# An FFT filter with a gated feed-forward: the inverse transform's first chunk opened a slot sooner, its rows in two parts, and fewer matmul columns

## The chip, the cores and the metric

The kernel runs on one core of a Trainium2 chip. The metric is the device time of one execution in microseconds (us); the time of a kernel is the median of its runs. The trace is that of one profiled execution, and its times count from the start of its span. Engines have short names: PE is the matmul engine (PEld its weight loads), DVE, ACT and POOL the vector, scalar and GpSimd engines, SP the engine that issues nearly all transfers.

## The reference, cut to what matters

```python
# x [1, 2048, 1024], w_r and w_i [2048, 513], w1 [1024, 3584], w2 [3584, 1024]
xn = _layernorm(x)
X = jnp.fft.rfft2(xn, axes=(-2, -1)) * (w_r + 1j * w_i)
s = jnp.fft.irfft2(X, s=(S, D), axes=(-2, -1))
h = _silu(jnp.einsum("bsd,df->bsf", xn, w1))
g = _silu(jnp.einsum("bsf,fd->bsd", h, w2))
return x + s * g
```

## The kernel before, in words

PE runs one long stream. First come the 112 tiles of the first feed-forward matmul (`mm1`, tile `pa`), then the second (`mm2`, tile `pb`, L584 to L586): seven products m of a Strassen-like scheme by eight row tiles j, each in two halves k of 21 matmuls of 512 columns. Every value is kept as two float16 halves, so each product is three passes: high by high, high by low, low by high. The spectral filter goes between these matmuls as background work. `work()` is called after each half of `mm2`; one such call is a slot here. In a slot the background list `bg` may take a step, then `wq` (`w2_gen`) prepares a piece of w2: a transfer into `jr`, a second one into a spare part of a `w` tile, an addition on POOL (L457), a split on ACT and DVE (L284, L287). A background step that yields `PAUSE` ends its slot; after other steps the list goes on while DVE's estimated clock is less than 1 us ahead of PE's. `defer(n, fn)` runs `fn` n ticks later; there is one tick a slot, ahead of its work.

The background around the change is, in order: `f_gen`, the filter along the sequence, sixteen units u, whose results `zq` go to DRAM as `zd[c]`, one quarter q after every four units (`low_z`, L1101 for even c, L1104 for odd c); `edge_gen`, which treats the columns that the units leave out, with nine fp32 matmuls into `eps` (L1231 to L1233), and writes `zps` through DRAM (L1287, L1285); `switch(B, open_i, 5, lag=2)`, which lets two slots go by, closes the filter's pool, calls `open_i` and then lets slots go by until the fifth `PAUSE` is spent; and `i_gen(c)` for c in `IORDER` = 1, 3, 0, 2, the four chunks of the inverse transform.

`open_i` calls `load_i(1)`: for an odd chunk four transfers of 512 KB bring `zd[c]` to the tile `zt`, two for each half of the partitions (L1308), then one brings the constants `kk` (L1312). `i_gen(1)` begins with `edge_in(1)`, a DVE copy of `zps` into the first column of every block of `zt` (L1319), and a `PAUSE`. Its steps i = 0 to 5 then interleave `mat(g)` (24 matmuls of 128 columns into `iu`, L1350, from `zt` and `kk`; for even chunks L1358), `post(g)` (ACT and DVE) and `split(g)`. `mat(0)` is emitted in step 0, `mat(1)` in step 1, `mat(2)` and `mat(3)` at the end of steps 1 and 2, after their `PAUSE`. Group g reads two of the eight blocks l of each row of `zt`. When all four are through, `load_i` of the next chunk is called and `mat2(p)`, p = 0 to 3, runs: 24 matmuls each into `id` (L1439), whose bank is read by `bfly(p)` (L1448 to L1453).

SP issues transfers in program order. The second matmul's rows `ht` are issued by the half, two at the start of each j: the second half of the tile two further on and the first half of the one after that. The lines that the prediction needs most:

```python
add(bg, switch(B, open_i, 5, lag=2))          # in the order loop
src = zd[c].rearrange("(m e) r q h x -> r m e (q h) x", e=2)      # load_i, odd c
nc.sync.dma_start(dst[64 * r:64 * r + 64, e], src[r, :, e])       # L1308
(nc.vector if c == IORDER[0] else nc.gpsimd).tensor_copy(zt[:, :, :, :, 0, 0], zps[:, :, c])   # L1319
for r, cols in enumerate((slice(0, 130), slice(0 if g == 0 else 127, 256))):                   # mat2
```

## Time and profile before

| | us |
|---|---|
| median of 3 runs | 1208.4 (1207.18 to 1208.95) |
| profiled execution, its own time | 1207.29 |
| span of its trace | 1205.5 |
| PE busy in the span | 1195.1 (99%) |
| DVE busy | 1009.7 (84%) |
| ACT busy | 511.6 (42%) |
| POOL busy | 210.2 (17%) |

The profiled execution lies 1.1 us below the median and 0.1 us above the fastest run; 1.8 us of it lie outside the span. PE busy is the union of its matmuls, whose recorded ends overlap, so a matmul's cost is read from the distance between starts, or from the chain view, which splits the time without overlap. A wait is the idle time of an engine ahead of an instruction, with what ended it.

### The profile page before, as it was taken

The page shows a single profiled execution, that of the slowest core. Times are in us where ns is not written, and L with a number is a line of the kernel's source. Part 1 is how long each engine was busy: PE and PEld are TensorE (multiplying, and loading weights), DVE is VectorE, ACT ScalarE, POOL GpSimd, SP SyncE. Part 2 cuts the span into 40 slices and gives each one's busy share as a digit, 9 for nine tenths or more (in the row PEclk, how much of TensorE's full clock was granted, in tenths as well). Part 3 has the DMA queues.
Part 4 walks back from the last instruction along what each step waited for, and adds up shares of the span by engine and source line. Part 5 has one row for each costly group of instructions (what it writes and reads, how often), then busy time and mean ns, then how long its engine had stood idle before and what let it go on. Part 6 is the DMA issues. An engine that isn't in the chain of part 4 may idle for free.

```text
span 1205.5 us, 18361 instructions
## 1 busy us (share of the span) xinstructions
PE 1195.1 (99%) x6600; PEld 597.1 (50%) x6600; DVE 1009.7 (84%) x1971; ACT 511.6 (42%) x698; POOL 210.2 (17%) x297
## 2 busy tenths in 40 slices
PE   8999999999999999999999999999999999999998
PEld 5544445444544544444444444445455545555555
DVE  7778986996799598669968999999279898998696
ACT  7775654366466463445524233132032222343212
POOL 2330041102402300411100111125031231100000
PEclk9999999999999999999999999999999999999999
DMA  8788698589989976889989999993997989989577
GB/s 263 182 192 213 199 268 242 173 248 281 294 251 278 275 227 197 195 197 205 183 234 246 284 239 261 237 305 131 261 333 219 367 308 329 363 319 343 175 242 267
DMA packets 279540, 302.24 MB, mean 251 GB/s; under 512 B 47956, under 2 KB 206932, under 8 KB 278548
## 3 DMA queue, kind: packets, MB, share of 16 engines
q1 hardware_dynamic: 275848, 291.69, 81.1%
q0 software_dynamic: 3312, 9.24, 4.5%
q8 instruction: 52, 0.85, 0.3%
q14 instruction: 40, 0.33, 0.1%
q10 hardware_dynamic: 288, 0.13, 0.0%
HBM read 183.94 MB, written 110.77 MB: 244 GB/s over the span
## 4 chain that ended last, share of the span: by engine, by line
PE 93%; DVE 3%; DMA 3%; issue 1%; SPq 1%; ACT 0%; POOL 0%; ACTq 0%; DVEq 0%
PE pa L500 48%; PE pb L584 12%; PE pb L585 12%; PE pb L586 12%; PE id L1439 2%; PE fx L1070 2%; DMA ht<-hd 2%; PE iu L1358 1%; PE iu L1350 1%; PE fa L837 1%; PE fa L838 1%; PE fa L839 1%; DMA w<-in_B_w_dram 0%; DVE Z L1192 0%; SPq L1104 0%
## 5 line engine op out<-in xcount | busy, mean ns | idle before, releaser
L500 PE MATMUL pa<-xnT,w 128*128 128x512 f16 x2688 | 584.0, 379 | 0.0
L500 PEld LDWEIGHTS <-w 128*128 128x128 f16 x2688 | 261.6, 98 | 311.9 <-issue 0.3
L584 PE MATMUL pb<-w,ht 128*128 128x512 f16 (+2 forms) x812 | 300.4, 372 | 1.0 <-DMA ht<-hd 1.0
L585 PE MATMUL pb<-w,ht 128*128 128x512 f16 (+2 forms) x812 | 300.4, 372 | 0.0
L586 PE MATMUL pb<-w,ht 128*128 128x512 f16 (+2 forms) x812 | 300.3, 372 | 0.0
L509 ACT ACTIVATE h<-pa,s 128x512 f32<-128x512 f32 x112 | 75.9, 681 | 153.4 <-PE pa L500 112.8
L586 PEld LDWEIGHTS <-ht 128*128 128x128 f16 x812 | 79.5, 98 | 91.0
L584 PEld LDWEIGHTS <-ht 128*128 128x128 f16 x812 | 79.5, 98 | 87.7 <-DMA ht<-hd 1.1
L585 PEld LDWEIGHTS <-ht 128*128 128x128 f16 x812 | 79.5, 98 | 86.5
L284 ACT ACTIVATE w<-jr,sc 128x512 f16<-128x512 f32 x98 | 67.5, 712 | 64.6 <-POOL jr L457 60.4
L287 DVE SCALAR_TENSOR_TENSOR hoone<-h,hs,hoone 128x2048 f16<-128x2048 f32 x28 | 65.6, 2342 | 17.0 <-ACT hoone L284 17.0
L287 DVE SCALAR_TENSOR_TENSOR w<-jr,sc,w 128x512 f16<-128x512 f32 x98 | 78.0, 803 | 0.0
L1192 POOL TENSOR_TENSOR Z<-yb 128x32 f32<-128x32 f32 x64 | 34.9, 573 | 224.9 <-DVE yb L1169 224.9
L284 ACT ACTIVATE hoone<-h,hs 128x2048 f16<-128x2048 f32 x28 | 55.9, 1997 | 18.4 <-DMA hd<-hoone 18.4
L457 POOL TENSOR_TENSOR jr<-jr,w 128x512 f32<-128x512 f32 x28 | 38.8, 1387 | 123.8 <-DMA w<-in_B_w_dram 75.9
L1092 ACT ACTIVATE zq<-Z,zs 128x1024 f16<-128x1024 f32 x16 | 18.4, 1148 | 91.5 <-DVE Z L1192 54.3
L287 DVE SCALAR_TENSOR_TENSOR hosum<-hr,hs,hosum 128x1536 f16<-128x1536 f32 x28 | 50.7, 1811 | 7.2 <-ACT hosum L284 7.2
L284 ACT ACTIVATE hosum<-hr,hs 128x1536 f16<-128x1536 f32 x28 | 43.9, 1569 | 20.5 <-DMA hd<-hosum 12.1
L539 DVE TENSOR_TENSOR hr<-h 128x1024 f32<-128x1024 f32 x28 | 34.1, 1218 | 18.3 <-ACT h L509 18.0
L678 ACT ACTIVATE pl<-pl,c 128x512 f32<-128x512 f32 (+2 forms) x28 | 17.4, 655 | 72.7 <-DVE pl L654 42.4
L284 ACT ACTIVATE w<-w1r,rs 128x1024 f16<-128x1024 f32 x28 | 32.0, 1143 | 27.8 <-DVE w L287 23.5
L1192 DVE TENSOR_TENSOR Z<-yb 128x128 f32<-128x128 f32 (+1 forms) x128 | 42.3, 398 | 0.0
(246 smaller groups left out, 1520.4 us busy)
## 6 DMA issues: line engine op xcount, KB each, us to landing
ht<-hd SPq DMA_DIRECT2D x112, 448.0 KB, 6.5
hd<-hoone SPq DMA_DIRECT2D x28, 1024.0 KB, 8.6
hd<-hosum SPq DMA_DIRECT2D x28, 768.0 KB, 5.5
w1r<-in_B_w_dram SPq DMA_DIRECT2D x28, 512.0 KB, 6.6
w2m<-in_B_w_dram SPq DMA_DIRECT2D x28, 512.0 KB, 6.4
jr<-in_B_w_dram SPq DMA_DIRECT2D x56, 256.0 KB, 6.2
ws<-wd SPq DMA_DIRECT2D x42, 256.0 KB, 4.4
jr<-ws SPq DMA_DIRECT2D x42, 256.0 KB, 6.2
```

What stands on the lines that cost most here:

```text
L284: nc.scalar.activation(hi, raw, AF.Copy, scale=scale)
L287: nc.vector.scalar_tensor_tensor(lo, raw, scale, hi, op0=OP.mult, op1=OP.subtract)
L457: nc.gpsimd.tensor_tensor(raw[n], raw[n], more.pop(n), op=OP.add)
L500: nc.tensor.matmul(ps, w[:, wh, d], xt[:, xh, d], start=(n == 0), stop=(n == 23))
L509: nc.scalar.activation(hq[:, 2 * (c % 2) + f % 2], ps, AF.Silu, scale=s1[:, f:f + 1])
L539: tt(sums[:, 0:2], hq[:, 0::2], hq[:, 1::2], op=OP.subtract)
L584: nc.tensor.matmul(ps, hh[:, 0], w[:, 0], start=first, stop=False)
L585: nc.tensor.matmul(ps, hh[:, 0], w[:, 1], start=False, stop=False)
L586: nc.tensor.matmul(ps, hh[:, 1], w[:, 0], start=False, stop=last)
L1070: nc.tensor.matmul(o, k[:, c, kh], v[:, c, vh], start=(n == 0), stop=(n == 2))
L1192: eng.tensor_tensor(Z[:, ns, pos], x0[:, :, ls], x1[:, :, ls], op=o_)
L1439: nc.tensor.matmul(ps[:, g, cols], us[g][:, uh, 4 * r + p], C["ci"][:, ch, g, r, cols], start=(r == 0 and n == 0), stop=(r == 1 and n == 2 ...
```

## The change

- The wait behind `open_i` is 4 in place of 5: the first chunk's `edge_in`, `mat(0)`, `mat(1)`, `mat(2)` with their `post` and `split` steps are emitted one slot sooner. `open_i` itself, and so the first load, stays in its slot.
- Behind step 2 of the first chunk stands one more `PAUSE`, so that `mat(3)` and all that follows keep their slots.
- `zd[c]` of an odd chunk is laid out with the two halves b of the eight blocks apart. It is written by four transfers a quarter as before, each now of one half h (runs of 512 bytes in place of 1024). `load_i` issues `kk` first, then four transfers of 256 KB for b = 0, and by `defer(2, ...)` four more for b = 1. Groups 0 and 1 read b = 0, groups 2 and 3 read b = 1; `edge_in` writes b = 0 only.
- `mat2` leaves out columns: 130 become 129 for groups 1 to 3 in the first row part, and the low constants' pass of group 0's second part has 129 in place of 256.
- The nine `eps` matmuls become three, of 72, 24 and 24 columns.

```diff
@@ -174,7 +174,7 @@
     rd = [[dp.tile([256, 1024], F32, name=f"rd{side}_{j}") for j in range(4)] for side in range(2)]
     rows4 = [[t.rearrange("(a c) (q r k) -> a c q r k", c=4, q=4, r=2) for t in half] for half in rd]
     axis = [dp.tile([2, 4096], F32, name=f"axis{c}") for c in range(2)]
-    zd = [dp.tile([128, 2, 4, 2, 512] if c % 2 else [128, 4, 2, 1024], F16, name=f"zd{c}") for c in range(4)]
+    zd = [dp.tile([128, 2, 2, 4, 2, 256] if c % 2 else [128, 4, 2, 1024], F16, name=f"zd{c}") for c in range(4)]
     zpd = dp.tile([128, 4, 2, 4, 2], F16, name="zpd")
     SETS = ("sum_0", "sum_1", "sum_d"), ("one_0", "dif_1", "dif_0", "one_3")
     hds = {(k, g): dp.tile([128, 4 * len(m), NP, 2, 128], F16, name=f"hd_{k}_{g}") for k, m in enumerate(SETS) for g in range(2)}
@@ -1100,8 +1100,9 @@
                 for c in range(0, 4, 2):
                     defer(1, lambda c=c: nc.sync.dma_start(zd[c][:, q], zv[:, :, c]))
                 for c in range(1, 4, 2):
-                    for r in range(2):
-                        defer(1, lambda c=c, r=r: nc.sync.dma_start(zd[c][:, r, q], zv[:, :, c, 512 * r:512 * r + 512]))
+                    for h in range(2):
+                        defer(1, lambda c=c, h=h: nc.sync.dma_start(
+                            zd[c][:, :, :, q, h].rearrange("m r b x -> m (r b) x"), zv[:, h, c].rearrange("m (k x) -> m k x", k=4)))
 
         load_w(0)
         high_v(0)
@@ -1227,10 +1228,11 @@
             g.tensor_copy(r0[:, n, 1:4], xv[:, n, 0, 3:0:-1])
         yield 1
         ps = pf.tile([128, 512], F32, name="eps", tag="ff")
-        for n in range(3):
-            nc.tensor.matmul(ps[:, n * 32 + 8:n * 32 + 32], perm[:, 0], rv[:, n, 1:4].rearrange("m q a r -> m (q a r)"), start=True, stop=True)
-            nc.tensor.matmul(ps[:, n * 32:n * 32 + 8], perm[:, 1], rv[:, n, 0].rearrange("m a r -> m (a r)"), start=True, stop=False)
-            nc.tensor.matmul(ps[:, n * 32:n * 32 + 8], perm[:, 2], r0[:, n].rearrange("m a r -> m (a r)"), start=False, stop=True)
+        p3 = ps[:, 0:96].rearrange("m (n x) -> m n x", n=3)
+        r3 = rv.rearrange("m n q a r -> m n (q a r)")
+        nc.tensor.matmul(p3[:, :, 8:32], perm[:, 0], r3[:, :, 8:32], start=True, stop=True)
+        nc.tensor.matmul(p3[:, :, 0:8], perm[:, 1], r3[:, :, 0:8], start=True, stop=False)
+        nc.tensor.matmul(p3[:, :, 0:8], perm[:, 2], r0.rearrange("m n a r -> m n (a r)"), start=False, stop=True)
         yield 1
         rr = piece(96).rearrange("m (n a r) -> m n a r", n=3, a=16)
         nc.scalar.activation(rr.rearrange("m n a r -> m (n a r)"), ps[:, 0:96], AF.Copy)
@@ -1300,23 +1302,29 @@
 
     def load_i(c):
         zt = C["p"].tile([128, 8192], F16, name=f"zt{c}", tag="zt", bufs=1)
+        k = C["p"].tile([128, 2064], F16, name=f"kk{c}", tag="kk", bufs=1)
         if c % 2:
-            src = zd[c].rearrange("(m e) r q h x -> r m e (q h) x", e=2)
-            dst = zt.rearrange("m (e k x) -> m e k x", e=2, k=8)
-            for r in range(2):
-                for e in range(2):
-                    nc.sync.dma_start(dst[64 * r:64 * r + 64, e], src[r, :, e])
+            nc.sync.dma_start(k, ki[c])
+            src = zd[c].rearrange("(m e) r b q h x -> r m e b (q h x)", e=2)
+            dst = zt.rearrange("m (e b x) -> m e b x", e=2, b=2)
+
+            def part(b):
+                for r in range(2):
+                    for e in range(2):
+                        nc.sync.dma_start(dst[64 * r:64 * r + 64, e, b], src[r, :, e, b])
+
+            part(0)
+            defer(2, lambda: part(1))
         else:
             nc.sync.dma_start(zt.rearrange("m (q h x) -> m q h x", q=4, h=2), zd[c])
-        k = C["p"].tile([128, 2064], F16, name=f"kk{c}", tag="kk", bufs=1)
-        nc.sync.dma_start(k, ki[c])
+            nc.sync.dma_start(k, ki[c])
         C["z"][c], C["k"][c] = zt, k
 
     def edge_in(c):
         zt = C["z"][c]
         if c % 2:
-            zt = zt.rearrange("m (e q h l i) -> m e q h l i", e=2, q=4, h=2, l=8)
-            (nc.vector if c == IORDER[0] else nc.gpsimd).tensor_copy(zt[:, :, :, :, 0, 0], zps[:, :, c])
+            zt = zt.rearrange("m (e b q h l i) -> m e b q h l i", e=2, b=2, q=4, h=2, l=4)
+            (nc.vector if c == IORDER[0] else nc.gpsimd).tensor_copy(zt[:, :, 0, :, :, 0, 0], zps[:, :, c])
         else:
             zt = zt.rearrange("m (q h r l i) -> m q h r l i", q=4, h=2, r=2, l=8)
             nc.gpsimd.tensor_copy(zt[:, :, :, :, 0, 0], zp[:, c].rearrange("m r q h -> m q h r"))
@@ -1329,7 +1337,7 @@
         yield PAUSE
         zt, k = C["z"].pop(c), C["k"].pop(c)
         if c % 2:
-            zt = zt.rearrange("m (e q h l i) -> m e q h l i", e=2, q=4, h=2, l=8)
+            zt = zt.rearrange("m (e b q h l i) -> m e b q h l i", e=2, b=2, q=4, h=2, l=4)
             k = k.rearrange("m (h y) -> m h y", h=2)[:, :, 0:1024].rearrange("m h (e q x) -> m e q h x", e=2, q=4)
         else:
             zt = zt.rearrange("m (q h r l i) -> m q h r l i", q=4, h=2, r=2, l=8)
@@ -1346,7 +1354,7 @@
                     for q in range(4):
                         o = ps[:, 512 * e + 128 * q:512 * e + 128 * q + 128]
                         for n, (zh, kh) in passes:
-                            lhs = zt[:, e, q, zh, ls].rearrange("m l i -> m (l i)")
+                            lhs = zt[:, e, g // 2, q, zh, slice(2 * (g % 2), 2 * (g % 2) + 2)].rearrange("m l i -> m (l i)")
                             nc.tensor.matmul(o, lhs, k[:, e, q, kh], start=(n == 0), stop=(n == 2))
                 return
             width, second = (129, 127) if c else (128, 128)
@@ -1434,8 +1442,9 @@
         def mat2(p):
             ps = pt.tile([128, 4, 256], F32, name=f"id{c}_{p}", tag="ft")
             for g in range(4):
-                for r, cols in enumerate((slice(0, 130), slice(0 if g == 0 else 127, 256))):
+                for r, span in enumerate((slice(0, 129 if g else 130), slice(127 if g else 0, 256))):
                     for n, (uh, ch) in passes:
+                        cols = slice(127, 256) if r and ch else span
                         nc.tensor.matmul(
                             ps[:, g, cols], us[g][:, uh, 4 * r + p], C["ci"][:, ch, g, r, cols],
                             start=(r == 0 and n == 0), stop=(r == 1 and n == 2), skip_group_check=True)
@@ -1509,6 +1518,8 @@
             if c == IORDER[0] and i == 1:
                 nc.sync.dma_start(C["ci"], ci)
             yield PAUSE if i <= 3 else 3.9
+            if c == IORDER[0] and i in (2,):
+                yield PAUSE
             if 1 <= i <= 2:
                 mat(i + 1)
         if c != IORDER[-1]:
@@ -1678,7 +1689,7 @@
                 max_job = add(xq, w2max_gen())
                 f_job = add(bg, switch(A, open_f, 1, max_job))
                 add(bg, f_gen())
-                add(bg, switch(B, open_i, 5, lag=2))
+                add(bg, switch(B, open_i, 4, lag=2))
                 for k in IORDER:
                     add(bg, i_gen(k))
             if left == 2 * LAST + 3:
```

## Rows read from the trace of the kernel before

**Rows 1.** The page's first part: busy time of each engine.

```profile
PE 1195.1 (99%) x6600; PEld 597.1 (50%) x6600; DVE 1009.7 (84%) x1971; ACT 511.6 (42%) x698; POOL 210.2 (17%) x297
```

**Rows 2.** Waits of PE, whole span: total us, times, longest us.

```profile
PE tp L805 <- ACT x L788: 1.6, 2, 1.4
PE tp L803 <- ACT x L788: 1.4, 1, 1.4
PE spin L1622 <- POOL ones L1614: 1.0, 1, 1.0
PE pb L584 <- DMA ht<-hd: 1.0, 1, 1.0
PE iu L1350 <- DMA kk<-in_kc_dram: 0.6, 1, 0.6
```

**Rows 3.** Stretches: us, busy PE, PEld, DVE, ACT, POOL (instructions), PEclk, DMA share, GB/s.

```profile
860.00:875.00 15.00, 15.00 (x71) 6.86 (x70) 1.35 (x2) 0.72 (x1) 1.05 (x1) 1.00 1.01 225
875.00:900.00 25.00, 23.49 (x180) 13.38 (x178) 18.06 (x41) 8.37 (x13) 8.23 (x6) 1.00 0.93 348
900.00:1100.00 200.00, 200.00 (x1272) 106.08 (x1271) 185.17 (x394) 60.22 (x114) 29.80 (x25) 1.00 0.90 320
```

**Rows 4.** Timeline of PE, 814 to 817: start us, us, line, [idle before, releaser].

```profile
814.70 0.30 PE L1231 MATMUL eps<-edge,perm 128*128 128x24 f32 x2
...
816.62 0.38 PE L584 MATMUL pb<-w,ht 128*128 128x512 f16 x1
```

**Rows 5.** Timeline of PE, 876 to 884: the first chunk's matmuls.

```profile
876.26 1.50 PE L1350 MATMUL iu<-kk,zt 128*128 128x128 f16 x24 [0.55 <-DMA kk<-in_kc_dram]
878.71 0.39 PE L584 MATMUL pb<-w,ht 128*128 128x512 f16 x1 [0.96 <-DMA ht<-hd]
...
883.26 1.50 PE L1350 MATMUL iu<-kk,zt 128*128 128x128 f16 x24
```

**Rows 6.** Chain that ended last, in pieces: start us, us, what.

```profile
813.55 1.31 PE fx L1070 x12
...
883.42 1.34 PE iu L1350 x24
...
926.86 1.53 PE id L1439 x24
```

**Rows 7.** Timeline of SP's issues, 846 to 866.

```profile
846.01 5.02 SPq L1104 DMA_DIRECT2D zd<-zq  x4
...
858.11 2.94 SPq L1308 DMA_DIRECT2D zt<-zd  x4
861.09 0.66 SPq L1312 DMA_DIRECT2D kk<-in_kc_dram  x1
...
865.55 2.58 SPq L560 DMA_DIRECT2D ht<-hd  x2
```

**Rows 8.** One line's issues and landings: L1308 (858 to 861), L560 (867.8), L447 (834.9).

```profile
L1308 SPq DMA_DIRECT2D zt<-zd x4: 476/594/1125, 858.1 to 859.9; - x4
...
DMA to landing us min/median/max: 9.6/12.4/15.2
...
L560 SPq DMA_DIRECT2D ht<-hd x1: 326/326/326, 867.8 to 867.8; - x1
DMA to landing us min/median/max: 12.0/12.0/12.0
...
L447 SPq DMA_DIRECT2D jr<-in_B_w_dram x1: 333/333/333, 834.9 to 834.9; - x1
DMA to landing us min/median/max: 3.1/3.1/3.1
```

**Rows 9.** Transfers in stretches 849:855, 326.4:328 and 862:872: packets, MB, mean rate.

```profile
DMA packets 1683, 2.33 MB, mean 388 GB/s; under 512 B 108, under 2 KB 1072, under 8 KB 1683
...
DMA packets 1031, 0.54 MB, mean 338 GB/s; under 512 B 3, under 2 KB 1026, under 8 KB 1031
...
DMA packets 322, 2.00 MB, mean 200 GB/s; under 512 B 60, under 2 KB 60, under 8 KB 97
```

**Rows 10.** Timelines of DVE and POOL, 837 to 876: the edge copy, one unit's Z.

```profile
875.51 0.21 DVE L1319 COPY zt<-zps 128x16 f16<-128x16 f16 x1 [12.02 <-DMA jr<-in_B_w_dram]
...
838.64 2.61 DVE L1192 TENSOR_TENSOR Z<-yb 128x128 f32<-128x128 f32 x8
...
837.49 2.23 POOL L1192 TENSOR_TENSOR Z<-yb 128x32 f32<-128x32 f32 x4 [0.74 <-DVE yb L1169]
```

## The prediction

> **What bounds the kernel now.** I read the busy times first: PE is busy 1195.1 of 1205.5 us and the next engine, DVE, 1009.7 [rows 1]. So the end moves only by PE work that goes and by PE idle time that goes. The list of PE's waits comes next: five entries. Three of them, 4.0 us, wait for the first layer norm and for the constant of the warm-up matmuls, which the change does not touch; the other two, 0.96 for `ht` and 0.55 for `kk`, are the only ones behind these [rows 2]. The timeline of PE puts both at one place, the first chunk of the inverse: `mat(0)` starts at 876.26 after 0.55 of idle time and the `pb` behind it at 878.71 after 0.96 [rows 5]. The stretches tell why: from 860 to 875 DVE works 1.35 us of 15 and ACT 0.72, while the DMA engines are taken all the time and yet move only 225 GB/s; from 900 on PE is full and DVE is at 185 of 200 [rows 3]. So there are three things to price: 1.51 us of idle time at 876, the matmul columns, and what moving `mat(0)` does at the place where the data are late.
>
> **Columns of `mat2`.** A matmul of 256 columns costs 1.31/12 = 109 ns in the chain, one of 128 columns 1.34/24 = 56 ns [rows 6], so 128 columns are 53 ns, 0.417 a column. One `mat2` loses 127 columns in one matmul and one column in nine, 136 columns, 57 ns. There are sixteen: **0.91 us**. `mat2` itself supports it: 3489 columns take 1.53 us [rows 6], 0.44 a column. PE is full around them [rows 3], so all of it reaches the end, unless DVE, which is at 93% there, becomes what PE waits for; today no PE wait names it [rows 2].
>
> The Trainium skill speaks against this term: TensorE: Matmul & The Clock Gate, section Back-to-back issue gap, gives a sustained spacing of about 81 ns at 128 columns and 131 at 512. By it 127 columns would be worth some 16 ns (my estimate from its two points), and the term 0.3 us. The trace disagrees, with 56 ns at 128.
>
> **Edge matmuls.** The nine fill PE from 814.70 to 816.62 [rows 4], 213 ns each whether 24 or 8 columns wide, so the fixed part sets their price. Three cost 0.64: **1.28 us** saved; were the one of 72 columns twice as dear, 1.07. I take 1.28. Their reader is POOL work that is not on the path.
>
> **The slot.** `mat(0)` was wanted when PE came free, at 876.26 - 0.55 = 875.7. A slot is 878.71 to 883.26, 4.55 us [rows 5], of which 0.02 is the reading. A slot sooner and with the edge saving ahead of it, PE comes free for it at 875.7 - 4.53 - 1.28 = **869.9**. The planner's condition does not hold it back: DVE does next to nothing in those slots [rows 3].
>
> When are its data there? The chain to them does not start at PE: before the rows can be read `zq` must be written, and SP's issues of that run from 846.0 on, with `zt` at 858.1 and `kk` at 861.1 [rows 7]. I assume that these times stay. The four `zt` pieces land 9.6 us after the first issue, at 867.7, to 15.2 after the last, at 875.1 [rows 8]: 2.46 us a piece of 512 KB, about 200 GB/s, as the packets of 862 to 872 also give [rows 9]. The edge copy then runs at 875.51, after DVE had waited 12.02 us, for 0.21 [rows 10]. `kk` comes in at about 876.2, where the stall ends, 1.1 us behind the last piece [rows 5].
>
> In the new order the queue turns to this load at 867.7 - 2.46 = 865.3. `kk` is first, 1.1; the four half pieces are 1.23 each, 4.9; the edge copy and what lies around it took 0.65 after the last landing. That makes 871.9. To it comes the price of the 512-byte runs: the window with the `zd` writes moves 388 GB/s, windows of nearly nothing but 512-byte packets 338 [rows 9], so the 1 MB of the last quarter takes 3.1 in place of 2.7 us, 0.4 more, on the path that sets `zt`'s issue; three earlier quarters are off it. This gives 872.3, and as the upper end 873, if the runs lose nearly three times that, since the window holds other packets too. Lower end: `kk` at 388 GB/s and half of `zt` at 213, from the issue at 858.1 on plus a lone landing of 3.1 [rows 8, 9], 868.1. Nearest is the loaded queue, since it is taken all through this stretch [rows 3]; I take **872.0**. PE, free at 869.9, then stands for 2.1 us, ends 0 to 3.1.
>
> **The `ht` stall.** The matmul that waited at 878.71 needs the transfer issued at 865.55, behind all of `zt` and `kk` [rows 5, 7]. Now half of `zt` lies behind it. It follows the half pieces (871.4), `jr` and `w`, and comes in at about 874 (the next `ht` landed at 867.8 + 12.0 = 879.8, so 1.1 a piece [rows 8]); it is wanted behind `mat(1)`, at 872.0 + 1.34 + 4.53 + 1.34 = 879.2. **0.96 is gone**, and so is the old 0.55. The second part of the rows is queued behind `ht`: 874 + 1.1 + 4.9, some 880 to 881; `mat(2)` wants it a slot behind `mat(1)`, near 883.8. The margin of 3 us is the cover of that step; without it each late us is a us.
>
> What else is queued: the edge copy now stands a slot sooner in DVE's order and holds the w2 split and an evacuation behind it until 872, as it held them until 875.5; PE did not wait for these then. The c = 3 load, 70 us later, is split as well; its first matmul then waited for nothing [rows 2]. The empty slot costs nothing on PE, which has `pb` in it.
>
> **Sum.** 0.91 + 1.28 + 0.96 + 0.55 - 2.1 = 1.6 us saved. The profiled execution of 1207.29 would become 1205.7; it lies 1.1 below the median, so the median of 1208.4 becomes **1206.8**. That is 0.13%, inside the 0.2% (2.4 us) that a measurement of this kernel can tell from no change. The point of it is that moving `mat(0)` takes back most of what the halved load gives.
>
> **Rivals.**
>
> *The rows are there when PE asks.* With data at 870 or sooner nothing is lost: 3.7 us, 1204.7; from 871.2 on downward the gain is over 2.4. For it: the half pieces are shorter packets and SP may be held less ahead of them. Against: the load in the queue from 846 on. The same time comes out if the change does not do what it says, the planner skipping a slot so that `mat(0)` stays where it was: wanted at 874.4, data at 872.0, no stall. Together 0.31.
>
> *The edge copy or `mat(0)` waits for both parts* (slower). The second part is issued ahead of the edge copy in program order, and lies between its rows in memory. If the dependence were drawn by spans, `mat(0)` would wait for 881 + 0.65, a stall of 11.7 us: 1216.4. It decides from a stall of 6.1 on (3.7 + 2.4). Against it: POOL's Z writes every eighth row between DVE's, is emitted behind them, and yet starts at 837.49, ahead of DVE's at 838.64 [rows 10], so interleaved regions are told apart. 0.04.
>
> *Each of the added transfers pays for itself* (slower). If the half pieces did not follow each other but each took near the 3.1 us of a lone 256 KB transfer [rows 8], part 0 would end 4 x 3.1 = 12.4 after 866.4, `mat(0)` at 879.5, a stall of 9.6, 1214.3. Against: in the loaded queue 448 KB follow in 1.1. 0.05. The Trainium skill has the rule behind this in SBUF — State Buffer, section The DMA setup-cost knee: about 2 us a transfer whatever its size; by its formula a half piece is 2.6 us, which would make it 1212. The trace agrees for a lone transfer and not for a queue of them.
>
> *Narrow matmuls save nothing.* If spacing hardly fell below 256 columns, 0.6 less, 1207.4. 56 against 109 ns speak against it. 0.04.
>
> **How the numbers follow.** Forecast, with stalls of 1.4 to 3.1 around it: 0.53. With the narrow-matmul rival the same side has 0.57. Faster 0.31; slower 0.04 + 0.05, and 0.03 for a second part that is late at `mat(2)` by more than 5 us over its margin: 0.12. The range takes in the case of no stall, with the 0.3 by which medians of three may lie lower, and on the other side a saving of nothing (873 and a share of the costs not seen) with the spread of 0.9 of the runs above: 1204.4 to 1209.3.
>
> **What would show it.** The time from the last `zq` write to `zt`'s issue about 0.4 longer; three `eps` matmuls in 0.64; `mat2` in 1.47; `mat(0)` at about 872 with PE idle some 2 us before it, and the edge copy its releaser; no idle time at the `pb` behind `mat(1)` or at `mat(2)`. I am wrong if `mat(0)` starts without a wait, if it waits past 873, or if PE waits at a place where it had none.

## The result, and the profile after

The changed kernel takes 1209.26 us (median of 18 runs, 1205.32 to 1215.03) where the kernel before takes 1206.53 beside it (18 runs, 1205.28 to 1209.46). The ratio is 1.0026 with an interval of 1.0018 to 1.0034: slower by about 3.1 us by the ratio (2.7 between the medians), where 1.6 us of gain were forecast. The median lies just under the upper end of the predicted range; the sign is wrong.

The profiled execution of after took 1209.53, its span is 1207.6, 2.1 longer than that of before. Its busy row, which answers to [rows 1]:

```profile
PE 1192.1 (99%) x6588; PEld 594.7 (49%) x6588; DVE 1007.4 (83%) x1971; ACT 511.7 (42%) x698; POOL 210.2 (17%) x295
```

and PE's waits, as in [rows 2]:

```profile
PE iu L1358 <- DVE zt L1327: 3.1, 1, 3.1
PE tp L805 <- ACT x L788: 2.5, 2, 2.3
PE id L1448 <- DVE us L1437: 1.5, 2, 1.0
...
PE id L1448 <- ACT us L1436: 0.9, 1, 0.9
```

PE's busy time is 3.0 us shorter, 0.9 of it in the first 16 us (12.00 before, 11.14 in after, for the same matmuls), and PE still ends later. The old waits for `kk` and `ht` [rows 2] are gone. Two kinds have come: one before `mat(0)` and three before `mat2`. The `tp` waits are in the first microseconds and end before the first `pa`, which starts at 15.9 in both traces. (Line numbers have shifted: `mat` is L1358 for odd chunks, the edge copy L1327, `mat2` L1448, the copies behind `mat` L1372 to L1375.)

The timeline of PE in after, the places that [rows 4, 5] showed of before, and those of the new waits:

```profile
814.65 0.34 PE L1233 MATMUL eps<-edge,perm 128*128 128x72 f32 x2
...
815.24 0.38 PE L584 MATMUL pb<-w,ht 128*128 128x512 f16 x1
...
872.85 1.50 PE L1358 MATMUL iu<-kk,zt 128*128 128x128 f16 x24 [3.06 <-DVE zt L1327]
874.18 0.38 PE L584 MATMUL pb<-w,ht 128*128 128x512 f16 x1
...
914.46 1.41 PE L1448 MATMUL id<-cis,us 128*128 128x130 f16 x20
916.36 1.88 PE L1448 MATMUL id<-cis,us 128*128 128x129 f16 x28 [0.49 <-DVE us L1437]
...
987.51 0.29 PE L1448 MATMUL id<-cis,us 128*128 128x129 f16 x2 [0.92 <-ACT us L1436]
988.77 1.88 PE L1448 MATMUL id<-cis,us 128*128 128x129 f16 x28 [0.97 <-DVE us L1437]
```

Three `eps` matmuls take 0.59 (815.24 - 814.65) where nine took 1.92. PE came free for `mat(0)` at 872.85 - 3.06 = 869.79 and stood until the edge copy was through. The `pb` behind `mat(0)` has no wait. The `mat2` waits are 0.49, 0.92 and 0.97, together 2.38. The account of the profiled execution: 3.06 + 2.38 lost, 1.51 of old waits and 2.19 of matmuls (the predicted 0.91 + 1.28) saved, 1.74 longer, of the 2.1 by which the span grew.

Where the `mat2` waits come from is read behind `mat(0)`, on ACT, DVE, POOL and SP. First ACT, then DVE and SP in after's timeline:

```profile
876.29 0.59 ACT L1372 ACTIVATE uc<-iu 128x512 f32<-128x512 f32 x1
884.99 0.72 ACT L284 ACTIVATE w<-jr,sc 128x512 f16<-128x512 f32 x1 [8.11 <-POOL jr L457]
885.61 0.58 ACT L1372 ACTIVATE uc<-iu 128x512 f32<-128x512 f32 x1
```

```profile
872.54 0.21 DVE L1327 COPY zt<-zps 128x16 f16<-128x16 f16 x1 [11.09 <-DMA jr<-in_B_w_dram]
...
886.22 0.69 DVE L1374 TENSOR_TENSOR ub<-iu,uc 128x512 f32<-128x512 f32 x1 [3.65 <-ACT uc L1372]
...
941.02 0.29 DVE L1488 TENSOR_TENSOR s<-spa 128x128 f32<-128x128 f32 x1 [9.03 <-DMA sd<-s]
```

```profile
845.66 5.74 SPq L1104 DMA_DIRECT2D zd<-zq  x4
...
858.39 0.38 SPq L1307 DMA_DIRECT2D kk<-in_kc_dram  x1
858.82 2.79 SPq L1314 DMA_DIRECT2D zt<-zd  x4
...
868.25 3.35 SPq L1314 DMA_DIRECT2D zt<-zd  x3
872.24 0.45 SPq L1314 DMA_DIRECT2D zt<-zd  x1
872.78 0.53 SPq L447 DMA_DIRECT2D jr<-in_B_w_dram  x1
873.41 0.38 SPq L452 DMA_DIRECT2D w<-in_B_w_dram  x1
```

Read it from the last row backwards. The second part of the rows, four transfers, is issued from 868.25 on; right behind it stand the two transfers of a w2 piece, `jr` and `w`. POOL's addition of that piece starts at 883.69, when `w` has landed (the chain below has it). ACT's split of the piece waits for the addition until 884.99, and in ACT's order the copy `uc` of `mat(1)`'s result stands behind that split. DVE, which needs `uc`, is idle for 3.65 us until 886.22. The chain that ended last, in order of time (start us, us, what), goes the same way:

```profile
862.38 10.97 DMA w<-in_B_w_dram
873.41 10.12 DMA w<-in_B_w_dram
883.69 1.27 POOL jr L457
...
915.75 7.34 DMA kk<-in_kc_dram
...
931.05 9.94 DMA sd<-s
...
987.49 1.24 DVE us L1437
988.77 1.88 PE id L1448 x28
995.18 1.47 PE id L1448 x24
```

It passes no matmul between 862 and 988: it runs by way of the w2 pieces, DVE and the next chunk's loads to the wait at 988.77. The waits at 987.51 and 988.77 are those of the second chunk, c = 3, whose own load is in two parts: the store `sd<-s`, issued at 931.05 right behind its second part, lands 9.94 later, and DVE is idle for 9.03 us until then (941.02). In before the same DVE work starts at 941.28 after 5.13 of idle time, so it comes no sooner in after, while that chunk's `mat2` is asked for at 985.30 in place of 994.03. In [rows 3] PE was full from 900 to 1100; in after, with the columns of rows 3,

```profile
860.00:875.00 15.00, 11.94 (x74) 5.99 (x73) 2.18 (x4) 0.72 (x1) 2.76 (x2) 1.00 1.03 265
875.00:900.00 25.00, 25.00 (x170) 13.51 (x169) 19.76 (x49) 9.00 (x14) 7.71 (x6) 1.00 1.00 319
900.00:1000.00 100.00, 97.62 (x643) 52.42 (x642) 89.00 (x198) 28.19 (x53) 21.56 (x17) 1.00 0.86 292
```

The idle time has moved from the second stretch into the first and third.

A second thing stands in these times. `mat2` is asked for sooner: the first `id` starts at 914.46 in after, at 919.0 in before. Counted in halves of `mm2` ahead of it, the first three `mat2` stand behind 58, 59 and 60 halves where they stood behind 59, 60 and 61, and later groups move by one or two halves as well. So the empty slot does not keep what follows in its slots, as the section on the change says: the list's condition on DVE's estimate lets later steps share slots, and they come sooner by themselves.

### The profile page after: what moved, and what is told of

Same layout as the page of the kernel before. It is cut to its first block, busy times and chain, and to the rows that moved or that the text cites. A ratio compares the mean times of both kernels' runs of the same rounds, so it can differ in the third digit from the quotient of the medians.

```text
span 1207.6 us, 18344 instructions
## 1 busy us (share of the span) xinstructions
PE 1192.1 (99%) x6588; PEld 594.7 (49%) x6588; DVE 1007.4 (83%) x1971; ACT 511.7 (42%) x698; POOL 210.2 (17%) x295
## 4 chain that ended last, share of the span: by engine, by line
PE 87%; DVE 6%; DMA 4%; issue 1%; SPq 1%; ACT 1%; POOL 0%; POOLq 0%; DVEq 0%; ACTq 0%
PE pa L500 48%; PE pb L586 11%; PE pb L584 11%; PE pb L585 11%; DMA w<-in_B_w_dram 2%; PE fx L1070 2%; PE id L1448 1%; PE iu L1366 1%; DMA sd<-s 1%; DVE uu L1407 1%; DVE w L287 1%; DMA jr<-in_B_w_dram 1%; DMA kk<-in_kc_dram 1%; PE fa L837 1%; PE fa L838 1%
## 5 line engine op out<-in xcount | busy, mean ns | idle before, releaser
L287 DVE SCALAR_TENSOR_TENSOR w<-jr,sc,w 128x512 f16<-128x512 f32 x98 | 75.5, 780 | 0.0
```

The costliest lines, as they stand in the source:

```text
L287: nc.vector.scalar_tensor_tensor(lo, raw, scale, hi, op0=OP.mult, op1=OP.subtract)
```

## The experiments

Two suspects were to be told apart: the slot (`mat(0)` sooner than its rows, and the new order of what follows, the "order" theory), and the rows in two parts (their price in the queue, or who waits behind them). The expectations name the theories by letters; the reading under each says what it decided. Each ratio is to the kernel before on the same chip, with its interval: 12 runs of each kernel (7 of the full rate) against 30 or 35 of before. Differences in us are worked out from the ratios; those between the medians differ from them by up to 0.8. In each kernel the line numbers shift a little.

**The slot taken back.** The changed kernel with the wait of 5 and without the empty slot; parts and matmuls stay.

```diff
-                add(bg, switch(B, open_i, 4, lag=2))
+                add(bg, switch(B, open_i, 5, lag=2))
-            if c == IORDER[0] and i in (2,):
-                yield PAUSE
```

> The changed kernel with the slot put back: the wait behind open_i is 5 again and there is no empty slot; the rows in two parts and the fewer matmul columns stay. In the order of PE's instructions the first chunk's groups then stand behind 51, 52, 53 and 54 halves of the second matmul, as in the kernel before, and all later groups too. Theory A (the loss comes from the slot alone: mat(0) is asked for before its rows are there, and the later groups stand one or two halves earlier than DVE can follow): no wait at mat(0), since PE asks at about 874.4 and the rows are there at 872.6; no wait at mat2; the whole 0.91 + 1.28 + 1.51 = 3.7 us is saved, 0.9969 of before. Theory B (PE's saved time is given back because DVE, 93% busy, is what mat2 waits for): PE still waits some 2 us at mat2, 0.999 of before.

Measured: 1209.55, ratio 1.0026 (1.0010 to 1.0041). Nothing came back, so the slot alone isn't the cause, against theory A; and theory B's 2 us of waits have come, but not at `mat2`, and with a longer time than its 0.999. `mat(0)` has no wait now, and others have come. PE's timeline in this kernel, then ACT's:

```profile
875.17 1.50 PE L1358 MATMUL iu<-kk,zt 128*128 128x128 f16 x24
...
887.49 1.50 PE L1358 MATMUL iu<-kk,zt 128*128 128x128 f16 x24 [0.41 <-DMA jr<-in_B_w_dram]
895.47 1.70 PE L1358 MATMUL iu<-kk,zt 128*128 128x128 f16 x24 [1.95 <-DVE ub L1375]
```

```profile
884.82 0.72 ACT L284 ACTIVATE w<-jr,sc 128x512 f16<-128x512 f32 x1 [8.66 <-POOL jr L457]
885.44 0.58 ACT L1372 ACTIVATE uc<-iu 128x512 f32<-128x512 f32 x1
```

With the order of before, `mat(0)`'s own copy `uc` now stands behind the late w2 piece: 885.44. ACT's timeline of the kernel before has it at 883.38:

```profile
883.38 0.58 ACT L1364 ACTIVATE uc<-iu 128x512 f32<-128x512 f32 x1
```

PE's stream starts 0.98 later in this execution (its first `pa` from `xnT` at 19.06, before 18.08), so the copy is better counted from the start of `mat(0)`: 885.44 - 875.17 = 10.27 behind it, where before had 883.38 - 876.26 = 7.12. `mat(3)`, which needs the buffer that `ub` reads, stands for 1.95. Behind that wait the granted clock is 0.50 from 896.66 to 900.05.

**The empty slot taken out.** The changed kernel without the added `PAUSE`.

```diff
-            if c == IORDER[0] and i in (2,):
-                yield PAUSE
```

> The changed kernel without the empty slot behind step 2; the slot sooner stays. mat(3) stands behind 53 halves, all later groups where the changed kernel has them. Theory A: the same wait of about 3 us at mat(0), waits of 1 to 3 us at mat2, within 1 us of the changed kernel, 1.0015 to 1.0035 of before. Theory C (the empty slot lets the planner's estimate of DVE fall back and so the later steps run ahead): the waits at mat2 go, 1.000 to 1.001 of before.

Measured: 1211.17, ratio 1.0031 (1.0016 to 1.0046). `mat(0)` waits 2.88, `mat2` 3.8 in all, and the granted clock is 0.50 from 991.65 to 995.00 (its profiled execution, 1213.9, is one of its longer ones). The empty slot is not where the time goes, as theory A had it: without it nothing comes back.

**The slot alone.** The kernel before with the wait of 4 and the empty slot.

```diff
-                add(bg, switch(B, open_i, 5, lag=2))
+                add(bg, switch(B, open_i, 4, lag=2))
+            if c == IORDER[0] and i in (2,):
+                yield PAUSE
```

> The kernel before with only the slot sooner and the empty slot; its rows come in one part, its matmuls are as they were. Theory A: PE asks for mat(0) at 871.2 and the rows are there at 876, a wait of about 5 us in place of 0.55; the wait of 0.96 for ht goes; waits of 1 to 3 us at mat2 as in the changed kernel: 5 to 7 us slower, 1.004 to 1.006 of before. Theory D (the loss comes from the halved rows and their traffic, not from the slot): within 0.2% of before.

Measured: 1211.08, ratio 1.0035 (1.0024 to 1.0047). PE waits once behind the warm-up, 3.8 us at `mat(0)`; no `mat2` waits, although the groups stand in the order of after (PE comes to the first `mat2` at 917.76 here, 3.3 later than in after; the full rate with the slot, below, shows the same without that). So the order by itself makes no `mat2` wait, and opening `mat(0)` ahead of its rows costs by itself, close to theory A's 1.004. The stall is not all: the clock granted to PE fell with it (timeline of PE, then a stretch with the columns of [rows 3]; 0.50 stands for the granted clock).

```profile
874.72 2.72 PE L1350 MATMUL iu<-kk,zt 128*128 128x128 f16 x24 [3.80 <-DMA kk<-in_kc_dram]
```

```profile
874.32:877.70 3.38, 2.98 (x26) 2.74 (x27) 1.16 (x2) 0.24 (x1) 1.27 (x1) 0.50 1.04 399
```

**The matmuls alone.** The kernel before with the skipped columns and three `eps` matmuls (those two parts of the diff, nothing else).

```diff
+                        cols = slice(127, 256) if r and ch else span
+        nc.tensor.matmul(p3[:, :, 8:32], perm[:, 0], r3[:, :, 8:32], start=True, stop=True)
```

> The kernel before with only the skipped columns of mat2 and the merged edge matmuls. Theory A: the 0.91 of mat2 is saved; the 1.28 of the edge matmuls is spent again at mat(0), whose rows do not come sooner, a wait of 1.8 in place of 0.55; 0.9 us saved, 0.9992 of before. Against it: both are saved, 2.2 us, 0.9982, and the wait at mat(0) stays 0.6.

Measured: 1206.81, ratio 1.0007 (0.9993 to 1.0022): no gain that can be told, nearer to theory A's 0.9992 than to the 0.9982 against it. The trace says where part of it goes: PE is at `mat(0)` sooner and waits 1.11 in place of 0.55 for the same rows, 0.97 for `ht` as before, and 0.40 at 1044. Of 2.2 some 1.2 is left in the profiled execution.

**The rows alone.** The kernel before with the new layout, `kk` first and the second part two ticks later; slot and matmuls as before.

```diff
+            part(0)
+            defer(2, lambda: part(1))
```

> The kernel before with only the rows in two parts (kk first, half of the rows, the other half two ticks later) and the layout that goes with it; slot and matmuls as before. Theory Q (what PE waits for from 870 on is set by the queue of transfers, and the second half of the rows now stands ahead of the w2 piece that POOL, then ACT, then the evacuation of mat(0) wait for): the old 1.51 us at mat(0) and ht go, but ACT's copy of mat(0) comes at about 885 and PE waits 1 to 2 us at mat(3), at times with the half clock behind it: 1.000 to 1.002 of before. Theory P (the waits of the run with the slot put back come only from PE being 2.2 us sooner): no wait, 0.9988.

Measured: 1209.8, ratio 1.0027 (1.0014 to 1.0039). By themselves the parts cost what the whole change costs. Its `mat(0)`, at 875.37, has no wait; `uc` of `mat(0)` starts at 884.03, and PE waits 0.93 at `mat(3)` and 0.89 at `mat2`, the places of theory Q. The profiled execution is the shortest of the twelve (1207.24) and its waits are only 0.3 more than the 1.51 of before; where the rest of the median's loss lies was not seen.

**The order of before with the rest of the change.** A second `PAUSE` puts the later groups back where they were.

```diff
-            if c == IORDER[0] and i in (2,):
+            if c == IORDER[0] and i in (2, 4):
```

> The changed kernel with one more PAUSE, behind step 4 of the first chunk: its first groups stay behind 50, 51, 52 and 54 halves, but all later groups stand where the kernel before has them (59, 60, 61, 64 and so on in place of 58, 59, 60, 63). Theory O (the waits at mat2 come from the later groups' earlier place): the waits at mat2 go, the wait of 3 us at mat(0) stays: 1.000 to 1.0015 of before. Theory Q (DVE is late from the first chunk on and stays so): some waits at mat2 stay, 1.002 and more.

Measured: 1210.14, ratio 1.0031 (1.0019 to 1.0042). The `mat2` waits go, and the time doesn't: `mat(0)` waits 4.03, and the clock falls under it. PE's timeline, then the stretch:

```profile
873.77 2.72 PE L1358 MATMUL iu<-kk,zt 128*128 128x128 f16 x24 [4.03 <-DVE zt L1327]
876.28 0.63 PE L584 MATMUL pb<-w,ht 128*128 128x512 f16 x1
876.71 0.63 PE L585 MATMUL pb<-w,ht 128*128 128x512 f16 x1
```

```profile
871.85:878.60 6.75, 4.83 (x30) 3.43 (x31) 2.75 (x6) 1.69 (x3) 1.69 (x1) 0.50 1.05 264
```

The 24 matmuls take 2.51 (876.28 - 873.77) in place of 1.33, and a `pb` matmul 0.43 in place of 0.22. PE comes to its first `mat2` at 922.26 here, a half of `mm2` (4.53) and 3.3 us more behind the 914.46 of after. So theory O isn't shown by the waits that went: PE was later by more than they were long.

**The second part behind the w2 piece, first attempt.** The kernel of the slot taken back, with the part one tick later.

```diff
-            defer(2, lambda: part(1))
+            defer(3, lambda: part(1))
```

> The changed kernel with the slot put back and no empty slot, and the second part of the rows deferred by three ticks in place of two, so that it is queued behind the w2 piece. Theory Q: that piece lands near 876 in place of 883, ACT copies mat(0) by 880, and the waits at mat(2) and mat(3) go; the second part lands near 884 and mat(2) asks at 887: 0.997 to 0.998 of before. Rival (the waits there are those of DVE's own work): as with two ticks, 1.0026.

Measured: 1209.75, ratio 1.0031 (1.0016 to 1.0047). A miss: SP's issues in its timeline stand as they stood, the part (866.52) still ahead of `jr` and `w` (871.41, 872.07), so it tests nothing that the kernel with two ticks does not. It is a second trace of the same order, though, with `mat(0)` at 874.03 and `uc` at 883.42, 9.39 behind it, and a wait of 1.62 at `mat(3)` (PE, then ACT, behind SP's lines).

```profile
866.52 4.48 SPq L1314 DMA_DIRECT2D zt<-zd  x4
...
872.07 0.34 SPq L452 DMA_DIRECT2D w<-in_B_w_dram  x1
```

```profile
874.03 1.50 PE L1358 MATMUL iu<-kk,zt 128*128 128x128 f16 x24
...
893.44 1.51 PE L1358 MATMUL iu<-kk,zt 128*128 128x128 f16 x24 [1.62 <-DVE ub L1375]
```

```profile
883.42 0.58 ACT L1372 ACTIVATE uc<-iu 128x512 f32<-128x512 f32 x1
```

**The same with four ticks.**

```diff
-            defer(2, lambda: part(1))
+            defer(4, lambda: part(1))
```

> The changed kernel with the slot put back and no empty slot, as before, and the second part of the rows deferred by four ticks; with three it was still issued ahead of the w2 piece, since that step of w2 issues nothing in the slot between. With four it is issued behind the piece and behind two more transfers of ht. Theory Q (the second part in front of the w2 piece makes ACT's copy of mat(0) late, and so DVE and mat(3)): the piece lands near 877 in place of 883, ACT copies mat(0) near 879.5 in place of 883.4, no wait at mat(3); mat(2) may wait up to 1 us for the second part: 0.997 to 0.999 of before. Rival (the waits behind mat(1) are not made by that piece): 1.002 to 1.003, as with two and three ticks.

Measured: 1206.35, ratio 0.9996 (0.9984 to 1.0007). Against 1.0026 with two ticks that is 0.3%, some 3.6 us (2.9 by the medians), for a change in the order of one queue: the part now stands behind the w2 piece and two transfers of `ht`. SP and ACT in its timeline:

```profile
868.56 0.33 SPq L452 DMA_DIRECT2D w<-in_B_w_dram  x1
...
871.44 3.26 SPq L1314 DMA_DIRECT2D zt<-zd  x4
```

```profile
877.83 0.58 ACT L1372 ACTIVATE uc<-iu 128x512 f32<-128x512 f32 x1
```

The w2 piece goes first, `uc` starts at 877.83, and the waits at `mat(2)` and `mat(3)` are gone. Beside the first attempt, with `mat(0)` at 874.02 here and 874.03 there, that is 5.59 sooner for the moved part alone. One of 1.13 at `mat2` is left: now the next w2 piece stands behind the part (ACT's next split waits until 886.55).

**The layout alone.** The new layout, all eight transfers at once, `kk` last; slot and matmuls as before.

```diff
+            part(0)
+            part(1)
+            nc.sync.dma_start(k, ki[c])
```

> The kernel before with only the new layout of the rows: written in runs of 512 bytes, read by eight transfers of 256 KB, all at once and kk behind them, in the order of the kernel before. Theory Q: the same bytes in the same order; kk lands 0.4 to 0.8 us later and mat(0) waits 1.0 to 1.4 in place of 0.55: 1.0003 to 1.001 of before. Rival (the shorter runs or the four added transfers are what costs, not the place of the second part): 1.002 and more.

Measured: 1206.01, ratio 0.9995 (0.9985 to 1.0005). Runs of 512 bytes and eight transfers for four cost nothing that can be told in the time; in the profiled execution `mat(0)` waits 1.13 in place of 0.55, as theory Q had it. The w2 piece stands behind all the rows here as in the rows alone, and ACT's split of it comes at 883.14 here and 883.40 there. What differs is `mat(0)`: at 876.66 here, at 875.37 there.

**Full rate.** The kernel before with the matmuls, and with the rows laid out so that one transfer of 2 MB fills all 128 partitions; `kk` behind it, slot as before, no parts.

```diff
-    zd = [dp.tile([128, 2, 4, 2, 512] if c % 2 else [128, 4, 2, 1024], F16, name=f"zd{c}") for c in range(4)]
+    zd = [dp.tile([2, 64, 2, 4, 2, 512] if c % 2 else [128, 4, 2, 1024], F16, name=f"zd{c}") for c in range(4)]
-                        defer(1, lambda c=c, r=r: nc.sync.dma_start(zd[c][:, r, q], zv[:, :, c, 512 * r:512 * r + 512]))
+                        defer(1, lambda c=c, r=r: nc.sync.dma_start(
+                            zd[c][r, :, :, q].rearrange("m e h x -> (m e) h x"), zv[:, :, c, 512 * r:512 * r + 512]))
-            for r in range(2):
-                for e in range(2):
-                    nc.sync.dma_start(dst[64 * r:64 * r + 64, e], src[r, :, e])
+            nc.sync.dma_start(zt, zd[c].rearrange("r m e q h x -> (r m) (e q h x)"))
```

> The kernel before with the fewer matmul columns and merged edge matmuls, and with the rows of odd chunks laid out so that one transfer brings all of them to all 128 partitions, in place of four to 64 each; one part, kk behind it, slot as before. Theory Q: the 2 MB take 5 to 6 us in place of 10, all that is queued behind comes 4 us sooner, no wait at mat(0), at the pb behind it, or at mat(3): 3.7 us saved, 0.997 of before. Rival (the rate of these rows is not set by the partitions they go to): as the matmuls alone, 1.000.

Measured: 1203.19 (7 runs, 1203.06 to 1204.10), ratio 0.9969 (0.9958 to 0.9980). It beats both kernels: 3.7 us under before (3.4 between the medians). PE waits for nothing after the warm-up. DVE's edge copy, ACT's `uc`, and the stretch of [rows 3]:

```profile
867.88 0.21 DVE L1317 COPY zt<-zps 128x16 f16<-128x16 f16 x1 [5.76 <-DMA zt<-zd]
```

```profile
876.45 0.58 ACT L1362 ACTIVATE uc<-iu 128x512 f32<-128x512 f32 x1
```

```profile
860.00:875.00 15.00, 15.00 (x82) 7.22 (x81) 3.53 (x6) 1.93 (x3) 2.50 (x3) 1.00 1.00 387
```

387 GB/s against 225 in the same stretch of before, with the transfer engines full in both (shares of 1.00 and 1.01): the load of four transfers to 64 partitions each kept them busy at half the rate. All rows are there at 867.88, sooner than the first half of them in after (872.54).

**Full rate with the slot.** The same with the wait of 4 and the empty slot.

```diff
-                add(bg, switch(B, open_i, 5, lag=2))
+                add(bg, switch(B, open_i, 4, lag=2))
+            if c == IORDER[0] and i in (2,):
+                yield PAUSE
```

> The run with the rows at full rate, with the slot sooner and the empty slot of the change added. There the rows and kk had landed by 869.2 and PE now asks for mat(0) at 869.9. Theory Q (the slot costs only because the rows are late): no wait of over 0.5 at mat(0), and since DVE is not late, none at mat2: 0.997 of before, as without the slot. Theory O (the later groups stand earlier than DVE can follow): 1 to 2.5 us of waits at mat2, 0.998 to 0.9995.

Measured: 1203.08, ratio 0.9971 (0.9962 to 0.9980). `mat(0)` starts at 869.5 without a wait, `mat2` waits nowhere, and the later groups stand as in after. So neither the slot nor the order costs anything once the rows are there, and the slot gains nothing either, as PE is full with or without it. This kernel is after with the rows loaded otherwise; its distance to after, 1.0026 to 0.9971, is what the late rows and what stands behind them cost there.

**Full rate alone.** As the full rate, without the matmuls.

```diff
-                        cols = slice(127, 256) if r and ch else span
+                for r, cols in enumerate((slice(0, 130), slice(0 if g == 0 else 127, 256))):
```

> The kernel before with only the rows of odd chunks at full rate; matmuls and slot as before. Theory Q: the two waits of 0.55 and 0.96 go, nothing else changes: 1.5 us saved, 0.9985 to 0.9988 of before, so that the matmuls' 2.2 us are the rest of the gain of both. Rival: the rows at full rate bring more than the two waits, because runs with late rows lose more than the profiled one shows: 0.9975 to 0.998.

Measured: 1205.05, ratio 0.9987 (0.9977 to 0.9996), about 1.5 us under before: the two stalls of [rows 2]. With the matmuls 3.7, so these are worth 2.2 where nothing takes them back: the predicted 0.91 + 1.28, though the two intervals leave more than 1 us to either side.

## Why the prediction was wrong, point by point

**The matmuls: right.** `mat2` takes 1.47 in after's chain, as predicted from 56 and 109 ns; `eps` 0.59 for 0.64; the difference of the two full-rate kernels is 2.2. The rule of the Trainium skill that was weighed against it (TensorE: Matmul & The Clock Gate, section Back-to-back issue gap: 81 ns at 128 columns) would have made them 0.3 + 1.28, an estimate from its two points, or 0.02 a `mat2`. The chain sides with the trace, 1.47 after 1.53; the run times are too rough to tell the two apart.

**When PE comes free and the old stalls: right.** 869.8 for 869.9; the waits of 0.55 and 0.96 are gone.

**When the data are there: 0.9 late.** The edge copy ran at 872.54 and `mat(0)` at 872.85, for 872.0 with bounds of 868.1 to 873. The stall is 3.06 for 2.1, within the 0 to 3.1 given, at its end. The load's first transfer was issued 12.7 behind the first of the last `zd` writes in place of 12.1 [rows 7], for the 0.4 that were put down to the short runs; the layout alone, though, cost nothing measurable in the time.

**Who waits behind the second part: the step that failed.** The prediction put the second part behind `ht` and asked only whether the part itself is in time for `mat(2)`: a margin of 3 us, "the cover of that step". That held: in after `mat(2)` waits for nothing. It did not ask who else stands behind 1 MB at 200 GB/s, some 5 us of the queue. The next w2 piece does, and by way of POOL, ACT's order and DVE the group's own evacuation does. The text had named the w2 split, but behind the edge copy on DVE, and closed it with "PE did not wait for these then"; so the sum has nothing for it. In before that piece stood in the queue behind all the rows too, and its split came at 882.75, `uc` of `mat(0)` right behind it. The halved load doesn't bring it forward: with the part ahead of it the split comes at 882.79 (first attempt), 883.40 (rows alone), 884.82 (slot taken back, started 0.98 later) and 884.99 (after). But PE is at `mat(0)` sooner, by 0.9 to 3.4 us. What is saved there is asked for again at the next place that needs the piece. The size of the wait goes with the distance of `uc` behind `mat(0)`, not with its time in the span:

| kernel | `mat(0)` starts | its `uc` starts | behind by | wait at `mat(3)` |
|---|---|---|---|---|
| slot taken back | 875.17 | 885.44 | 10.27 | 1.95 |
| first attempt (three ticks) | 874.03 | 883.42 | 9.39 | 1.62 |
| rows alone | 875.37 | 884.03 | 8.66 | 0.93 |
| before | 876.26 | 883.38 | 7.12 | 0 |
| layout alone | 876.66 | 883.76 | 7.10 | 0 |
| part last | 874.02 | 877.83 | 3.81 | 0 |
| full rate | 874.17 | 876.45 | 2.28 | 0 |

The rows with a wait put the limit at some 7.7 to 7.9 us (an estimate: 8.66 - 0.93, 9.39 - 1.62, and 10.27 less 1.95 and the 0.41 at `mat(2)`); before lies under it, which no wait of before could have shown.

In after, where `mat(0)` goes a slot sooner, `uc` of `mat(0)` slips in ahead of the late piece (876.29), that of `mat(1)` does not (885.61), and the loss comes out at `mat2`: 2.38 that stood in the sum at nothing, 0.49 in the first chunk and 1.89 in the second, which has a part of its own to wait behind. With the 0.96 at `mat(0)` that makes 3.3, all that lies between the forecast gain of 1.6 and the account's loss of 1.74. That the place in the queue causes it is shown for the kernel with the slot taken back, by moving the part alone (1.0026 to 0.9996). For after itself it is read from the chain view, and from the kernel with slot, order and fast rows, which has no such wait.

**"The empty slot costs nothing": right for the wrong reason.** It was said to keep what follows in its slots. It doesn't; the later groups came one or two halves sooner, and so `mat2` nearer to its late operands. Whether that adds to the waits is not shown. With the groups back in place the three waits are gone, but PE was 3.3 us later there, and the time is not gone; the slot taken back, the rows alone and the part last have the order of before and wait 0.2, 0.89 and 1.13 at `mat2`; with fast rows the order of after costs nothing.

**The rivals.** None of them happened. The nearest were the late second part, which was late for others and not for `mat(2)`, and the added transfers that pay for themselves, which the layout alone refutes. The rival that was missing is: whoever is queued behind the deferred part comes no sooner than before, or later, while PE does come sooner. By the rate of [rows 9] its upper end is the part's own 5 us in the queue, enough to turn the forecast's sign; part last, with the piece 5.6 us sooner, bears the size out.

**What stays open.** The account gives 1.7 of the 3.1 us of the ratio. The profile shows one execution. Falls of the clock would fit a part of the rest: four of the experiments' profiled executions have one (slot taken back, empty slot taken out, slot alone, order of before). But in 13 of after's 18 the mean granted clock was 0.998 or lower, as in 14 of the 100 of before that ran beside the experiments, and the medians of these 13 and of the other five are 1209.46 and 1209.15, so they don't account for the median; and the mean is a rough sign, 0.999 in the slot alone's profiled execution, which has a fall. Which waits the longer executions have was not seen. The same holds for the matmuls alone, the rows alone and the first attempt, whose profiled executions are shorter than their medians (1207.24 and 1208.45 for the last two, of 1209.8 and 1209.75). The table above shows where the waits come from, not the whole size of the ratios. With fast rows the spread goes too: 1202.85 to 1204.17 for the full rate with the slot, 1205.32 to 1215.03 for after.

## What to carry to other kernels

When a transfer is put off, list what is issued right behind its new place and follow each to the engine that waits for it, in that engine's own order; the transfer's own deadline is the smaller question. Having the first half of a load sooner does nothing for what stands behind the whole of it. Before splitting a load that is late, look at its rate: a load that keeps the transfer engines busy at half of what the stretches around it move is to be laid out anew; here neither halves nor slots were needed then. Starting work sooner than its operands gained nothing here, and an idle PE may be slower for a while afterwards.

## What the runs showed of the hardware that was not expected

**Half the partitions, half the rate.** Four transfers to 64 partitions each moved 200 GB/s [rows 9], one to all 128 brought the stretch to 387 GB/s. The Trainium skill states this in SBUF — State Buffer, section Door 1: The DMA port swizzle (why `[64,N]` ≈ `[32,N]`): 64 partitions in a row reach half of the ports. The trace agrees; the page's 196 GB/s for 1 MiB to partitions 0 to 63 lies near the 200 seen here. The full rate also makes one transfer of four; that the number isn't what counts is borne out by the layout alone, where eight for four cost nothing that can be told, but no run changes the partitions alone. The prediction took the 200 GB/s as given, and never asked why the rows moved at half the rate of what stood around them.

**The clock after an idle PE.** In the slot-alone and later-order kernels PE had stood since 870.9 and 869.7 when the granted clock went to 0.50, the lower of its two levels, 1.2 GHz, for the stretches shown (3.4 and 6.75 us), and the matmuls in them took nearly twice as long. Two more executions have such a stretch, behind a wait of 1.95 (slot taken back) and waits of 1.74 and 0.97 (empty slot taken out). In after PE stood 3.06 us at the same place, in the first attempt 1.62 at `mat(3)`, and the clock stayed at 1.00. Idle time of PE can thus cost more than its length, and it does not in every execution.

**An issue waits for a landing.** In the full stretch SP does not run ahead of the transfers. In before the first and the last of the four `zt` pieces land at 867.7 and 875.1 [rows 8], and the issues eight places behind them come at 867.81 and 875.19; in after the `w` issued at 862.38 lands at 873.35 (862.38 + 10.97 in the chain), and the `w` eight places on is issued at 873.41. So late rows hold back the issue of what follows and not only its data, and the chain goes from one `w` to the next. Whether the program or the queue makes it so, no run shows.
